# A linear-attention and Fourier kernel on one core: mirror comparisons from the fourth token tile on, weight stores in the tiles between, one transposition moved into the query product

## The chip, the core and the metric

The kernel runs on one core of a Trainium2 chip. The time is device microseconds of one execution on that core; lower is better. Engines are named as in the profile: PE is TensorE's matmul, PEld its weight load, DVE is VectorE, ACT is ScalarE, POOL is GpSimd, SP is the engine whose queue issues the DMAs. An engine works through its own instructions in order and waits, through semaphores, for those of others.

## The reference

`x` is 2048 x 640 in fp32. Four layers follow each other, each added to `x`: a Fourier layer, an attention layer, and both again with the same weights.

```python
def _A_ref(x, dft_seq_re, dft_seq_im, dft_hid_re, dft_hid_im):
    a = jnp.einsum("bsd,ed->bse", x, dft_hid_re)
    b = jnp.einsum("bsd,ed->bse", x, dft_hid_im)
    return jnp.einsum("ts,bse->bte", dft_seq_re, a) - jnp.einsum("ts,bse->bte", dft_seq_im, b)
...
def _B_ref(x, wqkv, wo):                       # 32 heads of 20
    q, k, v = ...                              # x @ wqkv
    phi = lambda t: jnp.where(t > 0, t + 1, jnp.exp(t)) + 1e-6
    pq, pk = phi(q), phi(k)
    kv = jnp.einsum("bhsd,bhse->bhde", pk, v)
    z = jnp.einsum("bhsd->bhd", pk)
    num = jnp.einsum("bhqd,bhde->bhqe", pq, kv)
    den = jnp.einsum("bhqd,bhd->bhq", pq, z)[..., None] + 1e-6
    ...                                        # (num / den) @ wo
x = x + _A_ref(_layernorm(x, axis=-1), ...)
x = x + _B_ref(_layernorm(x, axis=-1), wqkv, wo)
x = x + _A_ref(_layernorm(x, axis=-1), ...)
x = x + _B_ref(_layernorm(x, axis=-1), wqkv, wo)
```

The four DFT matrices are inputs. The kernel uses their symmetries, so it has to compare them with their own mirror images; if they don't match, it takes a general path instead, which is not run here.

## The kernel before, in words

`x` lies in SBUF as 16 token tiles of 128 rows. To keep fp32 precision, a factor is split into a high half (a cast on ACT, line 133) and a low half (a subtraction, on DVE or POOL, line 134), and a product is made of three matmuls: high by high, high by low, low by high (`product`, line 158).

A layer of attention runs in stages. `keys_values` (line 263) is the one that the change touches. Its loop over token tiles `n` does, for each tile: normalise the next tile (`normed`, line 212, with the scaling at line 127 on DVE); 30 matmuls for the keys (`proj(1, x)`, line 167); phi of the keys on ACT and DVE (lines 283 to 286) and their sum on POOL (line 298); the transposition of the next tile (`chunks`, five matmuls against the identity, line 139, then the split into halves, lines 133 and 134); 30 matmuls for the queries and phi of them. The keys of tile `n + 1` read the halves that `chunks` of tile `n` makes. The transposition stands between keys and queries, except where `got` is empty: then `query` runs it after the first two of five weight chunks, through `mid`. In the kernel before, that is so for tile 0 of layer 1 alone.

The loop runs over tiles 0 to 9, and then a gram pass over the same tiles follows: for each, 30 matmuls of normalised tokens by phi of the keys (`gram`, line 239, matmuls at line 251), whose operands `gram_ready` (line 229) makes one tile ahead: a normalisation and two splits, three DVE instructions a tile. Then the same for tiles 10 to 15. `combine` (line 368) follows, and `outputs`.

Between this work stand two side jobs.

`Check` (line 1010) makes the mirror comparisons. `fetch` loads up to four tiles of 344 or 346 KB (`ck<-in_ck`, line 1035, on SP) into the four buffers of the pool `raw`; `step` compares them on DVE (lines 1043 and 1060) and, with `more`, fetches the next. The buffers come free one by one as `step` goes on, so a fetch on SP waits for DVE. The first fetch is issued at the start of `keys_values`, when the weights of the layer, which use the same four buffers, are split. `STEPS` says in which token tiles and in which gram tiles a step stands, in both layers. The comparisons keep their program order on DVE; what else stands between them a scheduler decides, by priorities that `ahead` shifts.

`save` (line 207) writes the two halves of one weight chunk to DRAM, two stores of 320 KB on SP, so that layer 1 can load them instead of splitting again (`reload`, line 201). It is called in layer 0 alone, ten times: five chunks of the keys' weights, then five of the queries'. SP's instructions stay in program order, so a store stands behind the fetch that was issued before it.

Of the kernel before, what the change touches and what calls it, by code (L numbers as in the profile page):

```python
# [28 lines left out]
NE = 6  # L29
GA, GB = 384, 256  # L30
CUT = 10
STEPS = (0, 1, 2, 3, 4, 5, 6, 11, 12), (1, 3, 5, 7, 11)

START = 's0v s1v s2v s3v s4v r0p n2v n1v n0a n3v f0p f3p s7a k2p saa sba s9a k0v d0v s5v s6v f2v k3v d3v s8v d2v x12d d1p k1p f1v r1p n6v f6p e0v a0p b0v sda n4a n7v k7p n5v k5p k6p d5v c0v d7v k4v d4v d6v f5p r2p b1p nav kap n9v dap sfa nba dbv kbp n8a f7p f4v x03d x23d x13d x22d x02d f8v d8v a1v c1v k9p k8p f9p fap d9v b2v sca sea r3p fbv nev nfv fev a2v c2v x33a nca kcp fcv nda x32a w00a dfp dcp kfp kdp ffv fdv y32p kep dep a3v ddv v00v b3v c3v y33p t0p w12a w01a v01v v12v h3a l3v w10a v10v w02a t1p z0v v02v t3p t2p u20v u21v u22v u30v p0p w11a P0a m0v Q0v u31v u32v p1p v11p x01a y01p x11d x00a M0a N0v x10d y00v m1v'
SECOND = 'w02a sda x02d x12d x03d x13d x23a sev nea dev sfv nfa dfp nda kep kdp fdp fep x32a v02v ffv kfv y23v ddv y32v a3v x22a y22v b3p c3v h3a x33a w01a v01v y33v x10a y10v l3v t3p p1v m1p P1a w00a w10a w11a v10v u20v v11v u30v u21v u22v u31v x00d x01d M1a v00p w12a v12p x11a u32v y11p Q1p N1p'
# [114 lines left out]
def halves(pu):  # L150
    return pu.rearrange("p (a b) -> p a b", a=2)[:, :, :HD]


def h2(t):
    return t.rearrange("p (a b) -> p a b", a=2)


def product(nc, pu, sh, sl, wh, wl, hs=range(2), cs=None):
    n, m = len(sh), sh[0].shape[1]
    for c in range(n) if cs is None else cs:  # L160
        for s, w, first, last in (
            (sh[c], wh[c], c == 0, False),
            (sh[c], wl[c], False, False),
            (sl[c], wh[c], False, c == n - 1),
        ):
            for h in hs:
                nc.tensor.matmul(  # L167
                    pu[:m, 512 * h : 512 * h + HD], s, w[:, HD * h : HD * h + HD], start=first, stop=last
                )


class Attention:
# [90 lines left out]
    def keys_values(self, check=None, keep=1, saves=()):  # L263

        saves = list(saves)
        k, nc, W = self.k, self.k.nc, self.W
        pksum = k.temp()
        nc.gpsimd.memset(pksum, 0.0)
        self.PQ, late = {}, []
        if check is not None:  # L270
            check.fetch()

        def proj(part, x, mid=None):
            pu = k.psum()
            for cs in (range(ND),) if mid is None else (range(2), range(2, ND)):
                product(nc, pu, *x, [w[0] for w in W[part]], [w[1] for w in W[part]], cs=cs)
                if mid is not None and cs[0] == 0:
                    mid()
            return pu

        def phi(pu, out):
            e = k.temp()
            nc.scalar.activation(h2(e), halves(pu), AF.Relu, scale=-1.0)  # L283
            nc.scalar.activation(h2(out), halves(pu), AF.Relu)
            nc.scalar.activation(e, e, AF.Exp, scale=-1.0)  # L285
            nc.vector.scalar_tensor_tensor(out, e, 1e-6, out, op0=ALU.add, op1=ALU.add)  # L286

        x, acc, tail = self.x0, [], None
        for a, b in ((0, CUT), (CUT, NT)):
            pks = []  # L290
            for n in range(a, b):
                with k.ahead("normed", n + 1):
                    xn = self.normed(n + 1) if n + 1 < NT else None
                pk = self.slot()
                pu = proj(1, x)
                with k.ahead("key", n):
                    phi(pu, pk)
                nc.gpsimd.tensor_tensor(pksum, pksum, pk, op=ALU.add)  # L298
                pks.append(pk)
                def chunks(xn=xn, n=n):  # L300
                    tp = k.transposed(xn)
                    with k.ahead("chunks", n):
                        return k.split_chunks(tp)

                def query(i=self.order[n], x=x, mid=None):
                    pq = k.pqp.tile([128, D], F32, tag="pq", name=k.nm("pq"))
                    pu = proj(0, x, mid)
                    with k.ahead("query", i):
                        phi(pu, pq)
                    self.PQ[i] = pq  # L310

                got = []
                if xn is not None and (n or not k.layer):
                    got.append(chunks())
                if n < NT - keep:
                    query(mid=None if got or xn is None else lambda: got.append(chunks()))
                else:
                    late.append(query)
                if n > 0 and saves:
                    self.save(*saves.pop(0))  # L320
                if check is not None and n in STEPS[0]:
                    check.step(True)
                if n == b - 2:
                    with k.ahead("gram", a):
                        ready = self.gram_ready(a, pks[0])
                if xn is not None:
                    x = got[0]
            G = [k.psum() for _ in range(3)]
            tail = tail or k.psum()
            for n in range(a, b):  # L330
                with k.ahead("gram", n + 1):
                    nxt = self.gram_ready(n + 1, pks[n + 1 - a]) if n + 1 < b else None
                self.gram(G + [tail], ready, n == a, n == b - 1, a == 0)
                if n == CUT:
                    self.total(G, pksum)
                if check is not None and n in STEPS[1]:
                    check.step(n != STEPS[1][-1])
                ready = nxt
            if a == 0:
                acc = [self.slot() for _ in range(ND)]  # L340
                for c in range(ND):
                    (nc.scalar.copy if c % 2 else nc.vector.tensor_copy)(acc[c][:, :GA], self.place(G, c, 0))
                nc.scalar.copy(acc[ND - 1][:, GA:], self.place(G, ND - 1, 1))
        self.total_out(G)
        for c in range(ND):
            nc.vector.tensor_tensor(acc[c][:, :GA], acc[c][:, :GA], self.place(G, c, 0), op=ALU.add)
        c = ND - 1
        nc.vector.tensor_tensor(acc[c][:, GA:], acc[c][:, GA:], self.place(G, c, 1), op=ALU.add)
        for c in range(ND - 1):
            nc.scalar.copy(acc[c][:, GA:], self.place([None] * 3 + [tail], c, 1))  # L350
        self.combine(acc, late)
# [1002 lines left out]
```

## Time and profile before

| | us |
|---|---|
| runs of the kernel before | 807.38, 808.27, 809.39; median 808.27 |
| the profiled execution | 809.36, of which its span is 807.6 |
| layer 0, keys and queries of tiles 0 to 9 | 99.4 to 198.4 |
| layer 0, gram pass over them | 198.4 to 242.6 |
| layer 1, keys and queries of tiles 0 to 9 | 495.0 to 579.7 |
| layer 1, gram pass over them | 579.7 to 623.9 |

A row of a timeline has the start in us from the start of the span, the length, engine, line, operation, what it writes and reads, shape, count, and in brackets the idle time of the engine just before it with what ended it. A row of the chain of waits has start, length and what ran, or what was waited for. The rows themselves stand with the prediction.

### The profile page before, as it was taken

Reading aid. Unit: us, or ns where it says so; the run is one execution under the profiler, and the core shown is the slowest. Engines: PE = TensorE matmul, PEld = TensorE weight load, DVE = VectorE, ACT = ScalarE, POOL = GpSimd, SP = SyncE. Lnnn points to the kernel's source line nnn. Section 1 sums busy time; section 2 is a strip of 40 time slices with the busy share of each in tenths; the row PEclk is TensorE's granted clock in tenths of the full one; section 3 lists DMA queues with packets and bytes.
Section 4 is the critical chain, followed back from the end, with each engine's and each line's share of the span. In section 5 each row is a group of like instructions: output and inputs, shape, how many; then the busy total and the mean of one; then the engine's idle time right before and its main releaser. Section 6 shows DMA issues by size and latency. Waiting matters only on the chain.

```text
span 807.6 us, 12984 instructions
## 1 busy us (share of the span) xinstructions
PE 746.9 (92%) x4920; PEld 709.8 (88%) x4920; DVE 608.8 (75%) x1153; ACT 338.0 (42%) x592; POOL 319.1 (40%) x354
## 2 busy tenths in 40 slices
PE   0489998999999999999889999999999999999997
PEld 0138898999999999899885899999999999989997
DVE  7799887864982755999986789776597386499982
ACT  4534544355334453445563424544633445341110
POOL 4987981221021110469997656211101111134310
PEclk9989999999999999999999999999999999999999
DMA  8122416772360422000004652554044024001121
GB/s 320 64 79 73 130 57 195 248 222 105 107 204 4 141 82 80 16 8 1 1 1 134 210 174 97 176 157 141 1 140 140 1 71 143 21 12 50 66 83 70
DMA packets 36008, 81.25 MB, mean 101 GB/s; under 512 B 4142, under 2 KB 5937, under 8 KB 35936
## 3 DMA queue, kind: packets, MB, share of 16 engines
q1 hardware_dynamic: 35904, 80.27, 31.5%
q8 instruction: 41, 0.67, 0.4%
q14 instruction: 31, 0.25, 0.1%
q0 software_dynamic: 32, 0.06, 0.1%
HBM read 68.10 MB, written 11.80 MB: 99 GB/s over the span
## 4 chain that ended last, share of the span: by engine, by line
PE 64%; DVE 17%; POOL 11%; issue 3%; ACT 2%; DMA 2%; SPq 0%; DVEq 0%; POOLq 0%; ACTq 0%
PE ps L167 40%; PE ps L251 16%; PE ps L139 3%; PE ps L943 2%; PE ps L396 2%; DVE x L970 1%; DVE w L134 1%; DMA ck<-in_ck 1%; POOL ab L744 1%; POOL ab L619 1%; POOL t L440 1%; PE ps L898 1%; DVE junk L1060 1%; DVE t L134 1%; POOL ab L749 1%
## 5 line engine op out<-in xcount | busy, mean ns | idle before, releaser
L167 PE MATMUL ps<-w,t 128*128 128x320 f32 x2880 | 443.4, 312 | 8.9 <-DVE t L134 7.3
L167 PEld LDWEIGHTS ps<-w,t 128*128 128x128 f32 x2880 | 426.1, 189 | 11.8 <-DVE t L134 9.3
L298 POOL TENSOR_TENSOR t<-t,s 128x640 f32<-128x640 f32 x32 | 57.5, 1796 | 225.9 <-DVE s L286 217.9
L251 PE MATMUL ps<-t,t 128*128 128x256 f32 (+1 forms) x640 | 139.9, 309 | 0.0
L283 ACT ACTIVATE t<-ps 128x640 f32<-128x640 f32 x64 | 45.2, 706 | 162.2 <-PE ps L167 162.2
L1060 DVE CUSTOM_DVE_ANT_0 junk<-ck,ck 128x688 bf16<-128x688 f32 (+4 forms) x138 | 101.0, 732 | 10.4 <-DMA ck<-in_ck 8.6
L251 PEld LDWEIGHTS ps<-t,t 128*128 128x128 f32 x640 | 107.4, 188 | 0.0
L251 PE MATMUL ps<-w,t 128*128 128x384 f32 (+1 forms) x320 | 98.7, 310 | 0.0
L440 POOL TENSOR_TENSOR t<-pq,t 128x640 f32<-128x640 f32 x32 | 56.1, 1758 | 101.4 <-ACT t L366 48.5
L134 DVE TENSOR_TENSOR t<-ps,t 128x640 fp32r<-128x640 f32 (+1 forms) x66 | 53.9, 818 | 43.5 <-ACT t L133 43.2
L898 PE MATMUL ps<-cw,ab 128*107 128x512 f32 (+4 forms) x108 | 43.6, 544 | 33.6 <-DVE ab L639 27.0
L133 ACT CAST t<-ps 128x640 fp32r<-128x640 f32 (+1 forms) x66 | 45.6, 692 | 67.3 <-PE ps L139 58.8
L898 PEld LDWEIGHTS ps<-cw,ab 128*107 128x107 f32 (+1 forms) x108 | 19.0, 187 | 52.8 <-issue 50.3
L251 PEld LDWEIGHTS ps<-w,t 128*128 128x128 f32 x320 | 60.2, 188 | 0.2
L286 DVE SCALAR_TENSOR_TENSOR pq<-t,pq 128x640 f32<-128x640 f32 x32 | 27.2, 850 | 41.1 <-ACT t L285 41.1
L943 PE MATMUL ps<-t,u 107*128 107x322 f32 (+1 forms) x306 | 48.9, 315 | 3.2 <-DVE u L924 1.8
L943 PEld LDWEIGHTS ps<-t,u 107*128 107x128 f32 (+1 forms) x306 | 45.8, 190 | 5.6 <-DVE u L924 2.9
L139 PE MATMUL ps<-ident,t 128*128 128x128 f32 x320 | 45.6, 273 | 2.7 <-DVE t L127 1.2
L285 ACT ACTIVATE t<-t 128x640 f32<-128x640 f32 x64 | 48.0, 750 | 0.0
L127 DVE TENSOR_SCALAR t<-x,kept 128x640 f32<-128x640 f32 x58 | 44.6, 768 | 0.9 <-PE ps L251 0.9
L134 DVE TENSOR_TENSOR t<-t,t 128x640 fp32r<-128x640 f32 x32 | 26.4, 824 | 21.7 <-ACT t L133 21.3
L139 PEld LDWEIGHTS ps<-ident,t 128*128 128x128 f32 x320 | 38.2, 140 | 4.7 <-issue 1.5
(178 smaller groups left out, 992.6 us busy)
## 6 DMA issues: line engine op xcount, KB each, us to landing
ck<-in_ck SPq DMA_DIRECT2D x48, 346.0 KB
ck<-in_ck SPq DMA_DIRECT2D x48, 344.0 KB
save<-w SPq DMA_DIRECT2D x20, 320.0 KB
w<-save SPq DMA_DIRECT2D x20, 320.0 KB
x<-in_x SPq DMA_DIRECT2D x16, 320.0 KB
out<-x SPq DMA_DIRECT2D x15, 320.0 KB
raw<-in_wqkv SPq DMA_DIRECT2D x10, 320.0 KB
s<-in_wqkv SPq DMA_DIRECT2D x10, 320.0 KB
```

The costliest lines, as they stand in the source:

```text
L133: self.nc.scalar.copy(hi, src)
L134: self.engine(pool).tensor_tensor(lo, src, hi.bitcast(F32), op=ALU.subtract)
L139: self.nc.tensor.transpose(tp[:, 128 * c : 128 * c + 128], src[:, 128 * c : 128 * c + 128], self.ident)
L167: nc.tensor.matmul(pu[:m, 512 * h : 512 * h + HD], s, w[:, HD * h : HD * h + HD], start=first, stop=last)
L251: nc.tensor.matmul(self.place(G, c, part), x[:, 128 * c : 128 * c + 128], p[:, f : f + n], start=start and i == 0, stop=stop and i == 2, s ...
L283: nc.scalar.activation(h2(e), halves(pu), AF.Relu, scale=-1.0)
L285: nc.scalar.activation(e, e, AF.Exp, scale=-1.0)
L298: nc.gpsimd.tensor_tensor(pksum, pksum, pk, op=ALU.add)
L440: k.nc.gpsimd.tensor_tensor(t1, self.PQ[self.order2[n]], self.zb, op=ALU.mult)
L898: nc.tensor.matmul(pu[:m, o : o + n], e, w[:, f : f + n], start=g == 0 and i == 0, stop=g == end and not more and i == len(both) - 1,)
L943: self.k.nc.tensor.matmul(po[:, o : o + 322], s[:m, f : f + 128], w[:m, x, :], start=first, stop=last)
L1060: i = nc.vector.tensor_tensor_reduce(k.junk[:, : a.shape[1]], b, a, 1.0, 0.0, op0, op1, o)
```

## The change

The token tiles that carry a step of comparisons change from 0 to 6, 11 and 12 to 3 to 8 and 11 to 13, in both layers; the gram tiles with a step (1, 3, 5, 7 and 11) stay. The stores, until now in token tiles 1 to 10, go to token tiles 1, 2, 9, 10 and 14 and gram tiles 0, 2, 4, 6 and 8, one pair in each. In layer 0, as in layer 1 before, tile 0 no longer transposes tile 1 between its keys and its queries but inside the query product.

```diff
-STEPS = (0, 1, 2, 3, 4, 5, 6, 11, 12), (1, 3, 5, 7, 11)
+STEPS = (3, 4, 5, 6, 7, 8, 11, 12, 13), (1, 3, 5, 7, 11)
+SAVES = (1, 2, 9, 10, 14), (0, 2, 4, 6, 8)
...
                 got = []
-                if xn is not None and (n or not k.layer):
+                if xn is not None and n:
                     got.append(chunks())
                 if n < NT - keep:
                     query(mid=None if got or xn is None else lambda: got.append(chunks()))
                 else:
                     late.append(query)
-                if n > 0 and saves:
+                if n in SAVES[0] and saves:
                     self.save(*saves.pop(0))
                 if check is not None and n in STEPS[0]:
                     check.step(True)
...
                 self.gram(G + [tail], ready, n == a, n == b - 1, a == 0)
+                if n in SAVES[1] and saves:
+                    self.save(*saves.pop(0))
                 if n == CUT:
                     self.total(G, pksum)
                 if check is not None and n in STEPS[1]:
                     check.step(n != STEPS[1][-1])
...
+        assert not saves
         self.total_out(G)
```

## The prediction

> **What bounds the kernel now.** I read the page first, then busy time by stage, then TensorE's own timeline for its gaps, then what each gap waited for.
>
> ```profile
> span 807.6 us, 12984 instructions
> PE 746.9 (92%) x4920; PEld 709.8 (88%) x4920; DVE 608.8 (75%) x1153; ACT 338.0 (42%) x592; POOL 319.1 (40%) x354
> 99.39:198.40 99.01, 95.77 (x652) 94.98 (x652) 71.78 (x142) 44.28 (x70) 33.98 (x30) 0.98 0.55 172
> 198.40:242.60 44.20, 44.20 (x303) 44.10 (x302) 37.06 (x81) 17.92 (x28) 4.70 (x11) 1.00 0.49 143
> 495.00:579.70 84.70, 83.86 (x583) 83.79 (x583) 59.44 (x127) 41.22 (x65) 19.80 (x16) 1.00 0.39 118
> 579.70:623.90 44.20, 44.20 (x302) 44.13 (x302) 37.67 (x87) 17.92 (x28) 4.42 (x11) 1.00 0.43 128
> ```
>
> The stage rows give length, then busy time of PE, PEld, DVE, ACT and POOL, then the granted TensorE clock, the DMA share and GB/s. Rows one and two are layer 0's first ten token tiles and the gram pass over them, rows three and four the same of layer 1. All four are TensorE stages. Both gram passes have no gap; layer 1's token tiles have 0.84 us, at the very start, before anything the change touches. Only layer 0's token tiles lose something: 3.24 us of gaps, and a clock of 0.98. So that stage, 99 to 198 us, is where this change can win, and the other three are where it can lose.
>
> ```profile
> 99.39 4.65 PE L167 MATMUL ps<-w,t 128*128 128x320 f32 x30
> 105.27 0.74 PE L139 MATMUL ps<-ident,t 128*128 128x128 f32 x5 [1.22 <-DVE t L127]
> 105.76 9.09 PE L167 MATMUL ps<-w,t 128*128 128x320 f32 x60
> ...
> 141.28 5.62 PE L167 MATMUL ps<-w,t 128*128 128x320 f32 x26 [2.00 <-DVE t L134]
> 146.74 0.71 PE L139 MATMUL ps<-ident,t 128*128 128x128 f32 x5
> 147.20 9.01 PE L167 MATMUL ps<-w,t 128*128 128x320 f32 x60
> 156.04 0.71 PE L139 MATMUL ps<-ident,t 128*128 128x128 f32 x5
> ```
>
> Each row of five is the transposition of the next token tile; around it stand 30 key and 30 query matmuls. Between 147.20 and 156.04, 60 of them take 8.84 us, so 0.147 each, and a tile takes 9.3 us. Two gaps stand out: 1.22 us, where the second token tile isn't normalised yet, and 2.00 us, where the low half of a transposed tile isn't split yet. The 26 matmuls after the second gap take 146.74 - 141.28 = 5.46 us instead of 26 x 0.147 = 3.82: another 1.64 us. That is the clock:
>
> ```profile
> 101.61:105.02 3.41, 2.43 (x17) 2.17 (x15) 3.41 (x5) 0.89 (x2) 3.41 (x4) 1.00 0.38 106
> 139.16:142.57 3.41, 1.42 (x10) 1.29 (x10) 3.38 (x9) 1.50 (x3) 0.00 (x0) 1.00 0.82 264
> 142.57:145.99 3.42, 3.42 (x15) 3.42 (x14) 3.42 (x7) 0.00 (x0) 1.55 (x1) 0.50 0.76 190
> 391.74:395.16 3.42, 1.26 (x11) 1.00 (x9) 3.42 (x5) 1.04 (x3) 3.42 (x5) 1.00 0.00 0
> 395.16:398.57 3.41, 3.41 (x13) 3.41 (x14) 3.41 (x4) 2.23 (x5) 3.25 (x3) 0.50 0.00 0
> ```
>
> After a slice of 3.41 us with TensorE busy for only 1.42 (or 1.26) of it, the next slice is granted half the clock: 15 matmuls instead of some 23. The starts 142.57 and 395.16 lie 252.59 us apart, 74 times 3.413, so the slices seem to sit on a fixed grid. The slice with most of the 1.22 us gap was busy for 2.43 and cost no clock.
>
> Why was the split late?
>
> ```profile
> 134.75 0.70 ACT L133 CAST t<-ps 128x640 fp32r<-128x640 f32 x1
> 131.09 1.78 DVE L1060 CUSTOM_DVE_ANT_0 junk<-ck,ck 128x692 bf16<-128x692 f32 x1 [0.67 <-DMA ck<-in_ck]
> 138.68 0.88 DVE L1060 CUSTOM_DVE_ANT_0 junk<-ck,ck 128x692 bf16<-128x692 f32 x1 [1.86 <-DMA ck<-in_ck]
> 140.41 0.82 DVE L134 TENSOR_TENSOR t<-ps,t 128x640 fp32r<-128x640 f32 x1
> 149.53 0.82 DVE L134 TENSOR_TENSOR t<-ps,t 128x640 fp32r<-128x640 f32 x1
> 126.10 4.86 DMA ck<-in_ck
> 134.44 4.11 DMA ck<-in_ck
> ```
>
> The high half was cast by 135.45, but the low half began on DVE at 140.41, behind comparisons (L1060) that waited in order for their DMA. DVE had fallen behind at the start, and each late step fetched its successor late. One tile period on, at 149.53, the split is early enough for the key matmuls at 147.20 + 30 x 0.147 = 151.6, and no gap follows.
>
> **The change part by part.** *Transposition.* The order of instructions shows tile 1's five transposes after 14 query matmuls instead of before them; nothing is added.
>
> ```profile
> 103.29 1.83 DVE L127 TENSOR_SCALAR t<-x,kept 128x640 f32<-128x640 f32 x1
> 106.82 0.82 DVE L134 TENSOR_TENSOR t<-ps,t 128x640 fp32r<-128x640 f32 x1 [0.63 <-ACT t L133]
> 93.65 4.83 POOL L134 TENSOR_TENSOR w<-raw,w 128x640 fp32r<-128x640 f32 x3
> 102.97 1.79 POOL L134 TENSOR_TENSOR w<-raw,w 128x640 fp32r<-128x640 f32 x1
> ```
>
> TensorE finishes the keys at 104.04. The query weights of the first three chunks are split by 98.48 and the last at 104.76, before its turn, so it goes on at once; 14 matmuls later, at 106.1, the tile is long normalised (105.12). The 1.22 us go. Next in line is the split: transposed by 106.85, cast (0.70) and split (0.82) by 108.4. The keys of tile 1 start at 104.04 + 30 x 0.147 + 0.49 (the transposition, 105.76 - 105.27) = 108.9 and need the low half four matmuls later, at 109.5: 1.1 us of cover. If that cover were gone, up to 1.2 us return.
>
> *Comparisons.* Nine steps in layer 0's and layer 1's token tiles stay nine; they move from tiles 0 to 6, 11, 12 to tiles 3 to 8, 11, 12, 13.
>
> ```profile
> L1060 DVE CUSTOM_DVE_ANT_0 junk<-ck,ck 128x688 bf16<-128x688 f32 (+4 forms) x138 | 101.0, 732 | 10.4 <-DMA ck<-in_ck 8.6
> L1043 DVE TENSOR_REDUCE ca<-ck 128x1 f32<-128x344 f32 (+1 forms) x30 | 13.0, 433 | 0.0
> 111.70 0.49 DVE L106 BATCH_NORM_STATS2 st<-x 128x6 f32<-128x320 f32 x1 [2.18 <-POOL x L977]
> 119.21 0.80 DVE L134 TENSOR_TENSOR t<-ps,t 128x640 fp32r<-128x640 f32 x1
> ```
>
> A step is about 138/30 x 0.732 + 0.433 = 3.8 us of DVE. Without them in tiles 0 to 2, DVE is ahead from where POOL lets it go on (111.70). The tightest split there, now 119.21 to 120.01, loses two comparisons and the reduction ahead of it (1.9 us) and ends near 118.1; tile 2's keys start near 108.9 + 9.3 = 118.2 and need it 0.6 later. Thin, with some 0.7 us of cover; a miss costs up to 0.5. At tile 3 the first step's four raw tiles have been fetched since before tile 0, so the 2.00 us of waiting have no source; with them go the 1.64 us of half clock. From there each step has a whole tile period of 9.3 us, as tile 5 had when it caught up. Steps at tiles 7, 8 and 13 lie in stages with DVE idle for a quarter of the time or more (71.78 of 99.01 and 59.44 of 84.70): nothing; if a step there delayed a split, the nearest row is the gap of 2.00.
>
> *Stores.* Ten pairs of stores stay ten. On SP's queue two pairs (tiles 1 and 2) now stand right behind the first fetch, where SP waits for nothing and nothing behind them is due; two (tiles 9 and 10) stand where no fetch is near; the pair of tile 14 stands behind the fetch of tile 13's step and ahead of the loads of V's weights, which wait for TensorE anyway. Five pairs move into layer 0's gram pass, between the fetches. What they can cost is a fetch's landing in the gram pass, where DVE's queue is fuller:
>
> ```profile
> 198.47 44.06 PE ps L251 x300
> 212.74 0.33 SPq L1035 DMA_DIRECT2D ck<-in_ck  x1
> 213.36 0.50 DVE L1043 TENSOR_REDUCE ca<-ck 128x1 f32<-128x344 f32 x1
> 215.97 0.88 DVE L1060 CUSTOM_DVE_ANT_0 junk<-ck,ck 128x688 bf16<-128x688 f32 x1 [0.57 <-DMA ck<-in_ck]
> 217.29 0.82 DVE L134 TENSOR_TENSOR w<-s,t 128x640 fp32r<-128x640 f32 x1
> 221.82 0.51 DVE L1043 TENSOR_REDUCE ca<-ck 128x1 f32<-128x344 f32 x1
> ```
>
> A fetch alone lands in 215.97 - 212.74 = 3.2 us; the two in the chain above, with stores behind them, took 4.11 and 4.86. So a step may wait 0.9 to 1.6 us longer. A step's loop on DVE is 221.82 - 213.36 = 8.46 us, two gram tiles on TensorE are 8.81. With stores the loop is 9.4 to 10.1, so DVE loses 0.6 to 1.3 us in each of three loops, 1.7 to 3.8. The cover: the split at 217.29 ends at 218.11 and serves the sixth gram tile, which starts at 198.47 + 5 x 4.41 = 220.5: 2.4 us. Cost: 0 to 1.4; I take 0: of a step's four fetches only the last two have stores close behind, and the loop of 8.46 holds 0.57 of waiting already.
>
> *Sum.* 1.22 + 2.00 + 1.64 = 4.86 us. The profiled execution took 809.36 us (its span 807.6 and 1.8 around it), so it would take 804.5. The runs shown have a median of 808.27, 1.09 below, from 807.38 to 809.39, and may not all have paid the half clock: a gap of 2.00 us lies wholly inside one slice of 3.41 in (3.41 - 2.00)/3.41 = 41% of placements, and how much of it must lie inside isn't shown (between busy 1.42 and 2.43). I take half of 1.64 for the median: 808.27 - 3.22 - 0.82 = **804.2 us**. Bounds: 805.05 without the clock, 803.4 with all of it, and 802.6 if the other half-clock slice (395.16) also falls away by its place on the grid, worth about half of the 1.64 where DVE sets the pace. Upwards, 1.4 of the gram pass and part of the 0.5 of tile 2's split: 806.8. Range 802.6 to 806.8.
>
> [...]
>
> **The rivals.** *Stall moved:* the wait comes back at the new first steps, as the split at tile 3 still stands behind four wide comparisons on DVE. Then only the first gap goes: 808.27 - 1.22 = 807.05. Against it: the four raw tiles are there, and tile 5's row at 149.53. *Stores in the gram pass (slower):* if two stores behind a fetch double its landing to 6.5 us, the loop is 8.46 + 3.3 = 11.7, and three loops lose (11.7 - 8.81) x 3 - 2.4 = 6.4: 810.6 us. It decides against the change from a landing of 5.7 us (loop 10.96, loss 4.05); the rows with stores behind stop at 4.86. *Not what it says:* DVE is held at the start by POOL's residual sums (the 2.18 us before 111.70), not by comparisons, so nothing but order changes and both gaps stay in another form: 808.3. For it speaks only the thin cover at tile 2.
>
> **How the numbers follow.** Forecast 0.70, stall moved 0.13, no effect 0.09, stores 0.08. About 0.3% (2.4 us, so 805.85) is what a measurement of this kernel can tell from no change. Of the forecast's 0.70 some 0.64 lies below 805.85, and a part of the moved stall too if the clock slice goes: faster 0.68; same 0.25; slower 0.07.
>
> **What would show it.** No gap at tile 1's transposition; no gap and no half-clock slice between 130 and 150 us, so that the gram pass starts 4 to 5 us earlier, near 193.5; DVE's waits for ck gone from the token tiles. Wrong: a TensorE gap behind the splits of tiles 2 or 3, gaps in the gram pass behind the L134 splits with ck waits over 2 us, or new half-clock slices later that eat what was won.

## The result, and the profile after

The changed kernel takes 805.21 us (median of five executions, 803.95 to 805.39), the kernel before 808.27 (807.38 to 809.39). The ratio is 0.9945, with a 95% interval of 0.9929 to 0.9961: faster by about 0.5%. It is not the quotient of these two medians (0.9962); which executions it comes from isn't known here. Timed again, beside 31 executions of the kernel before with a median of 809.16 us, the changed kernel took 805.22 us, at a ratio of 0.9954 (0.9938 to 0.9971).

First the head of the page after, then busy time by stage of the profiled execution: layer 0's first ten token tiles, the gram pass over them, and the same two of layer 1. The columns are those of the prediction's stage rows.

```profile
span 803.5 us, 12981 instructions
PE 744.2 (93%) x4920; PEld 706.5 (88%) x4920; DVE 612.6 (76%) x1153; ACT 337.7 (42%) x592; POOL 317.7 (40%) x354
98.48:192.05 93.57, 93.57 (x651) 93.49 (x651) 64.42 (x127) 44.26 (x70) 33.66 (x30) 1.00 0.33 106
192.05:237.03 44.98, 44.53 (x302) 44.01 (x301) 39.05 (x86) 17.86 (x28) 5.58 (x11) 1.00 0.71 214
480.56:575.02 94.46, 93.62 (x652) 93.29 (x651) 62.79 (x137) 45.90 (x74) 27.49 (x34) 1.00 0.30 95
575.02:619.80 44.78, 44.54 (x303) 44.27 (x302) 39.82 (x89) 17.81 (x28) 5.29 (x11) 1.00 0.48 151
```

The third row begins at layer 1's first key matmul. In the kernel before, that matmul starts at 484.92 us, and not at 495.0, where the table of stages and the prediction's row for layer 1 begin; this is the kernel before from 484.92 on:

```profile
484.92:579.54 94.62, 93.78 (x653) 93.46 (x652) 69.52 (x152) 45.92 (x74) 27.99 (x34) 1.00 0.39 121
```

In the first stage TensorE is now busy for 93.57 of 93.57 us, at a clock of 1.00. From the first key matmul to the first gram matmul the kernel before took 98.92 us, so the stage is 5.35 us shorter. TensorE's own timeline shows both gaps closed:

```profile
98.48 6.76 PE L168 MATMUL ps<-w,t 128*128 128x320 f32 x44
105.08 0.71 PE L140 MATMUL ps<-ident,t 128*128 128x128 f32 x5
105.54 7.03 PE L168 MATMUL ps<-w,t 128*128 128x320 f32 x46
112.41 0.71 PE L140 MATMUL ps<-ident,t 128*128 128x128 f32 x5
...
131.12 0.71 PE L140 MATMUL ps<-ident,t 128*128 128x128 f32 x5
140.47 0.71 PE L140 MATMUL ps<-ident,t 128*128 128x128 f32 x5
```

The first transposition stands after 44 matmuls (30 keys, 14 queries), and from tile 2 on the tiles follow each other every 9.3 us with no bracket, so with no idle time. DVE's waits for ck in these tiles, 5.5 us in the kernel before, are gone.

The gram pass, without a gap before, has one now. The rows are of TensorE, of DVE, of the fetch (two issues, 214.6 and 215.0) and of the weight loads:

```profile
223.90 0.45 PE L252 MATMUL ps<-w,t 128*128 128x384 f32 x1 [0.36 <-DVE w L135]
221.69 0.88 DVE L1064 CUSTOM_DVE_ANT_0 junk<-ck,ck 128x688 bf16<-128x688 f32 x1 [3.69 <-DMA ck<-in_ck]
L1039 SPq DMA_DIRECT2D ck<-in_ck x2: 328/376/424, 214.6 to 215.0; - x2
197.32 0.19 PEld L252 LDWEIGHTS ps<-w,t 128*128 128x128 f32 x1 [0.35 <-DVE w L135]
```

DVE waited 3.69 us for a fetch that landed 221.69 - 215.0 = 6.7 us after its issue, and the split behind it came 0.36 us too late. In the second tile of the pass a weight load waited 0.35 us for a split, too. The pass grew from 44.06 to 44.98 us.

The two profiled executions differ by 807.6 - 803.5 = 4.1 us of span. By stage (before minus after): first matmul of the kernel 0.89 earlier; token tiles 5.35; gram pass -0.92; from there to layer 1's first key matmul 242.54 - 243.53 = -0.99; layer 1's token tiles 0.16; from its gram pass to the end -0.45.

### The profile page after: what moved, and what is told of

The parts are those of the page before. It is cut to its first block, busy times and chain, and to the rows that moved or that the text cites. A ratio compares the mean times of both kernels' runs of the same rounds, so it can differ in the third digit from the quotient of the medians.

```text
span 803.5 us, 12981 instructions
## 1 busy us (share of the span) xinstructions
PE 744.2 (93%) x4920; PEld 706.5 (88%) x4920; DVE 612.6 (76%) x1153; ACT 337.7 (42%) x592; POOL 317.7 (40%) x354
## 4 chain that ended last, share of the span: by engine, by line
PE 64%; DVE 21%; POOL 5%; DMA 3%; ACT 3%; issue 3%; SPq 0%; DVEq 0%; POOLq 0%; ACTq 0%
PE ps L168 44%; PE ps L252 13%; PE ps L140 3%; PE ps L947 3%; DVE w L135 2%; DVE t L135 2%; DVE junk L1064 1%; DMA ck<-in_ck 1%; DVE x L974 1%; DVE den L457 1%; POOL ab L623 1%; DVE t L461 1%; PE ps L400 1%; DMA rawc<-in_so 1%; DMA x<-in_x 1%
## 5 line engine op out<-in xcount | busy, mean ns | idle before, releaser
L1064 DVE CUSTOM_DVE_ANT_0 junk<-ck,ck 128x688 bf16<-128x688 f32 (+4 forms) x138 | 98.6, 714 | 7.3 <-DMA ck<-in_ck 5.5
L134 ACT CAST t<-t 128x640 fp32r<-128x640 f32 x32 | 23.3, 729 | 36.6 <-DVE t L128 31.8
```

What stands on the lines that cost most here:

```text
L134: self.nc.scalar.copy(hi, src)
L1064: i = nc.vector.tensor_tensor_reduce(k.junk[:, : a.shape[1]], b, a, 1.0, 0.0, op0, op1, o)
```

## The experiments

The theory was that three things add: the transposition closes the gap of 1.22 us, moving the comparisons off the first tiles closes the 2.00 us, and the half-clock slice goes with it. The rivals were that the stores behind the fetches made the split late, and that one gap was the other's echo. The table has each profiled execution's stages in us, cut at the first key matmul, the first gram matmul, the end of the gram pass and the same of layer 1; the last column is the ratio to the kernel before, timed beside it. Beside the experiments the kernel before had medians of 809.29, 809.16 and 809.90 us, so the ratios are not quotients with 808.27.

| | token tiles | gram pass | to layer 1's keys | its gram pass to the end | median | ratio (95%) |
|---|---|---|---|---|---|---|
| before | 98.92 | 44.06 | 242.54 | 228.04 | 808.27 | |
| changed | 93.57 | 44.98 | 243.53 | 228.49 | 805.21 | 0.9945 (0.9929 to 0.9961) |
| transposition alone | 96.91 | 44.16 | 243.39 | 227.87 | 808.20 | 0.9994 (0.9983 to 1.0006) |
| steps alone | 94.98 | 44.35 | 242.48 | 228.68 | 806.45 | 0.9967 (0.9954 to 0.9981) |
| stores alone | 97.18 | 44.07 | 243.38 | 228.46 | 810.13 | 1.0004 (0.9987 to 1.0021) |
| changed, stores off the gram pass | 93.58 | 44.34 | 243.06 | 228.53 | 804.39 | 0.9939 (0.9923 to 0.9955) |
| changed, again | 93.57 | 44.34 | 241.95 | 228.53 | 805.22 | 0.9954 (0.9938 to 0.9971) |
| early steps, no store near | 96.55 | 44.07 | 241.91 | 228.03 | 807.54 | 0.9978 (0.9964 to 0.9993) |
| changed, steps from tile 1 | 93.58 | 44.08 | 243.31 | 228.07 | 804.28 | 0.9940 (0.9919 to 0.9962) |
| changed, all stores in the gram pass | 93.58 | 44.60 | 242.71 | 228.62 | 805.74 | 0.9960 (0.9945 to 0.9976) |
| changed, first step in tile 0 | 94.89 | 44.05 | 242.51 | 227.97 | 805.57 | 0.9948 (0.9932 to 0.9963) |
| no step in tile 0, old transposition | 94.98 | 44.09 | 243.21 | 227.85 | 805.11 | 0.9950 (0.9936 to 0.9964) |
| two edits | 93.57 | 44.08 | 242.30 | 227.96 | 804.17 | 0.9939 (0.9923 to 0.9956) |
| steps from tile 1, stores off the gram pass | 93.57 | 44.08 | 242.97 | 227.90 | 804.48 | 0.9939 (0.9925 to 0.9954) |

### One part at a time

The transposition alone:

```diff
-                if xn is not None and (n or not k.layer):
+                if xn is not None and n:
```

> The kernel before with only the transposition of tile 1 moved into the query product. Theory (three causes add: the transposition pays for the gap of 1.22 us at 105 us, the moved comparisons for the gap of 2.00 us and the half-clock slice behind it): the gap at tile 1's transposition is gone, the gap behind the split at tile 5 and its late comparisons stay; 808.27 - 1.22 = 807.05 us, ratio 0.998 to 0.999. Rival (the start is what makes DVE late, and the gap at tile 5 is only its echo): with tile 1 transposed later, DVE is relieved, the gap of 2.00 us goes too, and the time is near that of the changed kernel, 805.2 us.

TensorE's timeline of that kernel:

```profile
105.23 0.71 PE L139 MATMUL ps<-ident,t 128*128 128x128 f32 x5
...
119.35 4.08 PE L167 MATMUL ps<-w,t 128*128 128x320 f32 x26 [1.07 <-DVE t L134]
...
140.10 4.07 PE L167 MATMUL ps<-w,t 128*128 128x320 f32 x26 [1.45 <-DVE t L134]
```

The gap at 105 us is gone, but a new one of 1.07 us stands behind the split of tile 2, and the one at tile 5 remains. Alone the edit gives nothing that can be measured (0.9994, the interval holds 1). Neither account had this: TensorE arrives earlier at a DVE that is just as late. That the gap at tile 5 remains refutes the account of it as an echo.

The steps alone:

```diff
-STEPS = (0, 1, 2, 3, 4, 5, 6, 11, 12), (1, 3, 5, 7, 11)
+STEPS = (3, 4, 5, 6, 7, 8, 11, 12, 13), (1, 3, 5, 7, 11)
```

> The kernel before with only the steps of the comparisons moved to tiles 3 to 8 and 11 to 13; stores in tiles 1 to 10 as before, the transposition as before. Theory (DVE's queue behind the early comparisons makes the split of tile 5 late): the gap of 2.00 us and its half-clock slice are gone, the gap of 1.22 us stays, and the gram pass has no gap, since no store stands in it; 808.27 - 2.00 - 0.82 = 805.45 us, ratio 0.9965. Rival (stores behind the fetches make the fetches land late, and that makes the split late): a gap of 1 to 2 us comes back at one of tiles 3 to 8, where fetches and stores still share the queue; 807 to 808.3 us.

The gap at tile 5 is gone with the stores of tiles 3 to 8 still behind the fetches; the gap at tile 1 (1.20 us here) is the only one between 100 and 190 us. The ratio of 0.9967 is what the theory gave (0.9965).

The stores alone (`SAVES` as in the changed kernel, the rest as before):

> The kernel before with only the stores moved (tiles 1, 2, 9, 10, 14 and gram tiles 0, 2, 4, 6, 8); steps in tiles 0 to 6, 11, 12 and the transposition as before. Theory (the early steps are the cause, the stores only add to the landing of a fetch): the fetches of tiles 3 to 6 land in about 3.2 us instead of 4.1 to 4.9, but the splits still wait behind comparisons; a gap of 0.5 to 2.0 us stays behind tile 4 or 5, the gap of 1.22 us stays too; 807 to 808.5 us, and a gap of up to 0.7 us in the gram pass. Rival (stores are the cause): no gap between 110 and 198 us but the 1.22, no half-clock slice there; 805.5 us.

```profile
140.32 4.08 PE L168 MATMUL ps<-w,t 128*128 128x320 f32 x26 [2.00 <-DVE t L135]
135.59:139.00 3.41, 2.73 (x19) 2.47 (x17) 1.40 (x5) 1.22 (x3) 0.00 (x0) 1.00 0.97 335
139.00:142.42 3.42, 2.10 (x14) 2.10 (x15) 3.42 (x9) 0.70 (x2) 0.65 (x1) 1.00 0.82 228
142.42:145.83 3.41, 3.41 (x27) 3.40 (x26) 3.38 (x6) 1.39 (x3) 0.91 (x1) 1.00 0.68 211
```

The first row is TensorE's, the others its clock slices. The same gap of 2.00 us stands in the same place, so moving the stores does nothing by itself. But the stores of tiles 1 and 2 still lie beside the early fetches here, so the run is no clean test of the rival. It prices the half clock instead: the gap falls on two of the slices of 3.41 us, busy for 2.73 and 2.10 us, neither costs any clock (1.00 in each and behind them), and the 26 matmuls behind it take 4.08 us where the kernel before took 5.62. The median of 810.13 us (807.39 to 812.48) lies above the 807 to 808.5 of the theory, but the kernel before took 809.29 (806.77 to 812.63) beside it, and the interval of the ratio holds 1; the profiled execution took 808.22.

The clean test: early steps and the old transposition, but no store before tile 7.

```diff
+SAVES = (7, 8, 9, 9, 10, 10, 13, 13, 14, 14), ()
...
-                if n > 0 and saves:
+                for _ in range(SAVES[0].count(n) if saves else 0):
                     self.save(*saves.pop(0))
...
```

> Comparisons in tiles 0 to 6, 11, 12 and the transposition of tile 1 as in the kernel before, but no store before tile 7 (one pair each in tiles 7 and 8, two each in 9, 10, 13, 14, none in the gram pass). Theory (the early steps keep DVE behind, whatever lies on the queue): the waits for ck among the comparisons of tiles 3 and 4 get shorter, by 1 to 2 us in sum, but a gap of 0.3 to 2.0 us stays at tile 4, 5 or 6, and the 1.22 us stay; 806.5 to 808.3 us. Rival (the stores near the fetches make the splits late): no gap behind a split between 110 and 198 us; 805.5 to 806.3 us.

```profile
105.46 0.74 PE L140 MATMUL ps<-ident,t 128*128 128x128 f32 x5 [1.19 <-DVE t L128]
...
140.63 4.09 PE L168 MATMUL ps<-w,t 128*128 128x320 f32 x26 [1.29 <-DVE t L135]
```

DVE's waits for ck in these tiles add up to 3.9 us, against 5.5 in the kernel before, as forecast. The gap is 1.29 instead of 2.00 us. So the early steps make a gap with no store near. Whether the other 0.71 us belong to the stores isn't shown by one execution each: the run of the stores alone had 2.00 us, the transposition alone 1.45.

### Which of the early steps

The changed kernel with its steps in tiles 1 to 6 and 11 to 13:

> The changed kernel with the steps in tiles 1 to 6 and 11 to 13 instead of 3 to 8 and 11 to 13; stores and transposition as in the changed kernel. Theory (what makes the split late is what DVE has to do while it catches up after the residual sums, so a step in tiles 1 and 2 is already too early): a gap of 0.5 to 2 us behind the split of one of tiles 2 to 5 comes back; 806 to 807.5 us. Rival (it is tile 0's step alone, or the number of steps, that matters): no gap, 805.2 us.

The theory falls: no gap, 93.58 us, as with steps from tile 3. Steps in tiles 1 and 2 were not too early. Then tile 0's step is left. Two runs look at it from both sides: tile 0's step put back, with the others late,

```diff
-STEPS = (3, 4, 5, 6, 7, 8, 11, 12, 13), (1, 3, 5, 7, 11)
+STEPS = (0, 3, 4, 5, 6, 7, 11, 12, 13), (1, 3, 5, 7, 11)
```

> The changed kernel with its first step back in tile 0 and the others in tiles 3 to 7 and 11 to 13. It parts what tile 0's step does by its own work on DVE from what it does through the fetches behind it. Theory (its comparisons fall into the time in which DVE and GpSimd still finish the residual sums, and push the split of tile 2; the gap at tile 5 is a second thing, made by late fetches of the steps that follow at once): a gap of about 1.0 us behind the split near 118 us, as with the transposition moved alone (1.07), and none at tiles 4 to 6; 805.2 + 1.0 = 806.2 us. Rival (only the run of steps from tile 0 on is too much, one step there is harmless): no gap between 100 and 198 us; 804.3 to 805.2 us.

and tile 0's step alone taken away, with the stores and the transposition as in the run of the stores alone (steps in tiles 1 to 6 and 11 to 13):

> The kernel with steps in tiles 1 to 6 and 11 to 13 and the stores of the changed kernel, but with tile 1 transposed between keys and queries as before. Beside the run with the stores moved alone it differs only in tile 0's step; beside the run with steps from tile 1 only in the transposition. Theory (two separate gains, one in front of the other): the gap of 1.2 us at 105 us stays and is the only one up to 198 us; 804.3 + 1.2 = 805.5 us. Rival (the transposition's 1.2 us only shift TensorE against DVE and are absorbed later): the gap is there, but the gram pass starts no later after the first key matmul than with the transposition moved; 804.3 us.

With tile 0's step put back, TensorE's gap and DVE's queue ahead of it are these:

```profile
119.45 4.08 PE L168 MATMUL ps<-w,t 128*128 128x320 f32 x26 [1.09 <-DVE t L135]
113.44 1.66 DVE L287 SCALAR_TENSOR_TENSOR pq<-t,pq 128x640 f32<-128x640 f32 x1
115.03 0.32 DVE L1047 TENSOR_REDUCE ca<-ck 128x1 f32<-128x173 f32 x1
115.27 0.86 DVE L1064 CUSTOM_DVE_ANT_0 junk<-ck,ck 128x692 bf16<-128x692 f32 x1
...
116.26 0.82 DVE L1064 CUSTOM_DVE_ANT_0 junk<-ck,ck 128x692 bf16<-128x692 f32 x1
...
118.59 0.80 DVE L135 TENSOR_TENSOR t<-ps,t 128x640 fp32r<-128x640 f32 x1
```

The same stretch of DVE in the changed kernel, whose first key matmul is 0.23 us earlier:

```profile
113.19 1.66 DVE L287 SCALAR_TENSOR_TENSOR pq<-t,pq 128x640 f32<-128x640 f32 x1
...
116.59 0.81 DVE L135 TENSOR_TENSOR t<-ps,t 128x640 fp32r<-128x640 f32 x1
117.32 0.82 DVE L287 SCALAR_TENSOR_TENSOR s<-t,s 128x640 f32<-128x640 f32 x1
```

One reduction and two comparisons stand ahead of the split: 118.59 - 116.59 - 0.23 = 1.77 us, enough for a gap of 1.09 at tile 2, and no gap follows at tile 5. Taking tile 0's step away brings 97.18 - 94.98 = 2.20 us, all of the gap at tile 5, while the 1.20 at tile 1 stay. With it go all of DVE's waits for ck in the token tiles. The first row is from the run of the stores alone (total, number, longest wait); the run without tile 0's step has no such row. The second is TensorE's only gap in that run between 100 and 190 us:

```profile
DVE junk L1064 <- DMA ck<-in_ck: 5.1, 6, 1.5
104.50 0.74 PE L140 MATMUL ps<-ident,t 128*128 128x128 f32 x5 [1.20 <-DVE t L128]
```

So tile 0's step does two things: by its own work it pushes the split of tile 2, and at the head of an unbroken run of steps it makes the later fetches late enough for a gap at tile 5. Whether taking out another step of that run would close the gap at tile 5 as well, no run shows. The transposition's price, with nothing late behind it, is 94.98 - 93.58 = 1.40 us. These prices rest on the stages of single traces. The ratios of whole executions can't tell these kernels apart: 0.9948 and 0.9950 for the two runs above, whose stage is 1.3 and 1.4 us longer than that of the changed kernel, 0.9945 and 0.9954 for the changed one.

### The stores in the gram pass

Two pairs in each of tiles 1, 2, 9, 10 and 14, none in the gram pass, the rest as in the changed kernel (`SAVES = (1, 1, 2, 2, 9, 9, 10, 10, 14, 14), ()`):

> The changed kernel with two pairs of stores in each of tiles 1, 2, 9, 10 and 14 and none in the gram pass. Theory (stores behind the fetches make the gap of 0.36 us at 224 us in the gram pass): that gap is gone and a fetch there lands in about 3.2 us again; 805.21 - 0.4 to 0.7 = 804.5 to 804.8 us. Rival (that gap comes from where the steps stand, since the first gram step now follows steps at tiles 7 and 8): it stays, 805.2 us. Against both: four stores in a row at tile 1 or 2 hold the first fetch or a load of weights back, and a new gap appears there; over 805.5 us.

The changed kernel once more:

> The changed kernel once more, for a second profile and for times on the same chip as the next three. Theory (the gap of 0.36 us at 224 us in the gram pass comes from the two stores behind a fetch, and so belongs to the kernel, not to one execution): a wait for ck of 2 us or more and a gap of 0.2 to 0.8 us near 224 us again; 805.2 us. Rival (an accident of one execution): no gap there. The two gaps of 0.75 and 0.80 us between 427 and 443 us, where a part of the gain was lost, come back if they belong to the kernel and not to the execution.

All ten pairs in the gram pass, two behind each fetch (`SAVES = (), (0, 0, 2, 2, 4, 4, 6, 6, 8, 8)`):

> The changed kernel with all ten pairs of stores in the gram pass, two pairs behind each fetch in gram tiles 0, 2, 4, 6 and 8, none in the token tiles. It prices the rival of the prediction (stores in the gram pass lengthen the fetches). Theory (only the fetch that is issued just ahead of the stores, one of the four of a step, lands late, and DVE's queue gives back part of it): the longest wait for ck grows from 3.7 to 6 to 7.5 us and the gaps in the gram pass from 0.36 to 3 to 5 us; 807.5 to 810 us. Rival of that (the stores take bandwidth from every fetch, as the prediction's rival had it: each of three loops loses): waits for ck of over 5 us in three steps, gaps of 10 us or more; over 814 us. Third (the gap does not come from the stores): no change, 805.2 us.

Without stores the gap is gone, the waits for ck add up to 0.8 us, and 804.39 us is close to what the theory gave. But it is gone from the second execution of the changed kernel as well; there the same fetch kept DVE waiting 1.30 us. And with twice the stores TensorE has no gap either, and the time is 805.74 us, not 807.5 or more. The waits of these two kernels on DVE, the changed one again and the one with all stores in the pass:

```profile
220.26 0.88 DVE L1064 CUSTOM_DVE_ANT_0 junk<-ck,ck 128x688 bf16<-128x688 f32 x1 [1.30 <-DMA ck<-in_ck]
```
```profile
210.71 0.88 DVE L1064 CUSTOM_DVE_ANT_0 junk<-ck,ck 128x688 bf16<-128x688 f32 x1 [0.55 <-DMA ck<-in_ck]
221.02 0.88 DVE L1064 CUSTOM_DVE_ANT_0 junk<-ck,ck 128x688 bf16<-128x688 f32 x1 [1.60 <-DMA ck<-in_ck]
230.45 0.87 DVE L1064 CUSTOM_DVE_ANT_0 junk<-ck,ck 128x688 bf16<-128x688 f32 x1 [2.00 <-DMA ck<-in_ck]
```

So the 0.36 us were a chance of one execution. Stores made fetches late: in the seven traces with stores in the pass DVE's waits for ck from 193 to 245 us add up to 2.2 to 4.7 us, in the seven without to 0.6 to 1.1. How late differs from one execution to the next: 4.7 and 2.7 us in the two of the changed kernel. The pass covered single waits of up to 2.37 us (the run without tile 0's step) with no gap of TensorE, and all but 0.36 of the 3.69. What does belong to the kernel is smaller. The five runs whose last early step stands in tile 8 have 44.34 us or more, the others 44.05 to 44.16 with or without stores: some 0.27 us, for the weight load that waits in the pass's second tile. The kernel with its first step in tile 0, which differs from the changed one only in that tile 8's step stands in tile 0, is among the others (44.05). From layer 1's gram pass on, the same five take 228.49 to 228.68, the others 227.85 to 228.07, except the stores alone (228.46).

### Joined variants

Two edits on the kernel before, the stores untouched:

```diff
-STEPS = (0, 1, 2, 3, 4, 5, 6, 11, 12), (1, 3, 5, 7, 11)
+STEPS = (1, 2, 3, 4, 5, 6, 11, 12, 13), (1, 3, 5, 7, 11)
...
-                if xn is not None and (n or not k.layer):
+                if xn is not None and n:
```

> The kernel before with two edits only: tile 0's step moved to tile 13 and the transposition of tile 1 moved into the query product; stores in tiles 1 to 10 as before, and so behind the fetches. Theory (tile 0's step and the transposition are all that the change needed): no gap between 100 and 198 us but at the very start, none in the gram pass; 804.3 to 805.2 us, ratio 0.994 to 0.9955. Rival (the stores had to move too, since they lengthen the fetches: without a store near, the gap at tile 5 was 1.29 instead of 2.00 us): a gap of 0.3 to 1.0 us behind the split of tile 3, 4 or 5; 805.5 to 806.2 us.

Steps from tile 1 joined with the stores off the gram pass:

> Steps in tiles 1 to 6 and 11 to 13, the transposition moved, and two pairs of stores in each of tiles 1, 2, 9, 10 and 14, none in the gram pass: the two variants that came out lowest, joined. Theory (nothing is left to win in these stages, as both already ran without a gap between 100 and 242 us): 804.3 us, no faster than either. Rival (the stores cost something still in the gram pass, and the later steps in the token tiles): 803.5 us or less. Against both: four stores behind the fetch of tile 1's step make the comparisons of tile 2 late, and a gap comes back at tile 3 or 4; over 805 us.

Both have 93.57 and 44.08 us, TensorE has no gap in either stage once the keys have begun, and both times lie within 0.2 us of the theory's. The two edits alone take 804.17 us, the lowest median of all: the stores did not have to move. By its interval (0.9923 to 0.9956) it can't be told from the changed kernel; by the stages of the traces it is 0.3 to 0.9 us shorter in layer 0's gram pass and 0.5 us shorter from layer 1's gram pass on.

## Why the prediction was right, and where it was not

*Direction and place* were right: the stage of layer 0's token tiles carries the gain, both named gaps are closed, and so is the half-clock slice. The stage gained 5.35 us where the sum had 4.86. Its terms, as the runs part them in the order stores, tile 0's step, transposition (they add up to the whole by construction): 1.40 for the transposition (1.22 forecast), 2.20 for the split at tile 5 (2.00), and, for the half clock (1.64), 98.92 - 97.18 = 1.74 between the kernel before and the one with the stores alone, which has the same gap at full clock; 5.62 - 4.08 = 1.54 of it stand in the 26 matmuls behind the gap. The first two are each 0.2 us more than the gap that they close. The clock term was paid in the trace of the kernel before, where the gap left a slice with 1.42 us of matmuls, and not in that of the stores alone, where it left slices of 2.73 and 2.10; so half of it was a guess about chance, and no run counts how often an execution pays it.

*That each term can be had by itself*, as the experiments' theory read the sum, was wrong; the sum holds because the change makes all its edits at once. The 1.22 us of the transposition can only be had once tile 0's step has moved; alone, the gap comes back as 1.07 us at tile 2. This is the prediction's rival of the moved stall, in another tile and for one half of the change. The cover that the prediction called thin there, 0.7 us, is the reason, and it was sized well: with tile 0's step back TensorE was ready at 119.45 - 1.09 = 118.36 us, which is 118.13 on the changed kernel's time, and there the split ended at 117.40. Two comparisons and a reduction ahead of the split (1.9 us by the prediction, 1.77 measured) use these 0.73 us up.

*"Each late step fetched its successor late"* was right as a chain: the waits for ck of 5.1 us go with tile 0's step alone. The prediction reasoned as if tiles 0 to 2 all had to be free; freeing tile 0 was enough.

*The stores.* The prediction moved them at no cost in the token tiles and took 0 of 0 to 1.4 in the gram pass. Without stores in it the pass took 44.34 us; with them one execution of the changed kernel took 44.34, the other 44.98, and the one with twice as many 44.60: 0 to 0.64, within the bounds. The rival's 6.4 us failed at its factor: a landing of over 5.7 us, from which it was to decide, did occur (6.7), but in one of three loops, and not in every execution. With it one of the prediction's own signs of being wrong appeared, a gap in the gram pass behind a wait for ck of over 2 us, and it cost 0.36 us.

*"Steps at tiles 7, 8 and 13: nothing"* failed. The idle quarter of DVE that it leaned on is an average over the stage and says nothing of its border (and tile 13 lies in neither of the two stages that it quotes). A step in tile 8 delays operands of the gram pass, 0.27 us in layer 0. In layer 1 the five traces with such a step, and no others, show TensorE waiting 0.24 to 0.26 us for a split there, and about 0.5 us more from there on. The row of the changed kernel:

```profile
580.49 0.44 PE L252 MATMUL ps<-w,t 128*128 128x384 f32 x1 [0.24 <-DVE w L135]
```

*What was given back.* Between the gram pass and layer 1 the profiled execution was 0.99 us slower than before. TensorE's timeline there, of the changed kernel and then of its second execution:

```profile
424.14 2.80 PE L902 MATMUL ps<-cw,ab 128*107 128x512 f32 x6 [1.53 <-DMA cw<-in_co]
427.74 7.97 PE L902 MATMUL ps<-cw,ab 128*107 128x512 f32 x18 [0.80 <-DMA cw<-in_so]
...
442.03 0.95 PE L902 MATMUL ps<-ch,tl 128*107 128x512 f32 x3 [0.75 <-DVE tl L800]
```
```profile
424.67 10.52 PE L902 MATMUL ps<-cw,ab 128*107 128x512 f32 x24 [1.80 <-DMA cw<-in_co]
...
440.65 0.95 PE L902 MATMUL ps<-ch,tl 128*107 128x512 f32 x3
```

The same kernel took 243.53 and 241.95 us for this part, and the other kernels lie between 241.91 and 243.39, in no order with their edits. So the part varies by 1.6 us from execution to execution, and the change has no share in it that these runs could show. What decides a landing or a late DVE there stays open.

*The level.* 804.2 us were forecast and 805.21 measured. The sum for the median left out the tile-8 steps (0.27 and about 0.5) and took half of the clock slice, of which the trace of the kernel before shows the whole (5.62 us for 26 matmuls) and that of the stores alone nothing (4.08); the rest lies within the spread of the executions. As a ratio the forecast is 804.2 / 808.27 = 0.9950, between the two that were measured. A match this close is in part luck: the two profiled executions differ by 4.1 us, where the sum for them was 4.86, and 0.89 us gained before the stage and 0.49 more in it than the sum partly cancel the 0.92 and 0.99 lost behind it.

## What to carry to other kernels

A gap's width is what its removal brings only if the next engine in the chain is not late as well: look at when the late engine would deliver for a consumer that arrives earlier. When several pieces of side work sit in a busy start, move the first one before moving all; here one step and one transposition held the whole gain, and the pieces that went further than needed took a little of it back at the next stage's border. Before explaining a gap below 1 us, take a second trace of the same kernel.

## What the runs showed of the hardware

*The half clock went with the gap's place in its slice, and its price with the stage.* In the trace of the kernel before, the granted clock falls to 0.50 twice between 100 and 800 us, at 142.57 and at 395.16, 252.59 us or 74 times 3.413 apart; in that of the first step in tile 0, at 391.49 and at 415.38, 23.89 us or 7 times 3.413 apart. A gap of 2.11 to 2.18 us stands in layer 0's outputs in nine traces, ahead of a group of 26 matmuls that begins between 389.50 and 395.10 us. In four of them the 26 take 5.60 to 5.63 us (before, steps alone, early steps with no store near, steps from tile 1), in five 4.08 or 4.09 (changed, changed again, transposition alone, stores off the gram pass, all stores in it). These are slices of 3.41 us, each with the slice behind it, from four kernels: changed, steps from tile 1, first step in tile 0, and stores off the gram pass.

```profile
388.00:391.41 3.41, 1.91 (x13) 1.91 (x14) 3.41 (x4) 1.20 (x3) 3.33 (x4) 1.00 0.00 0
391.41:394.82 3.41, 3.30 (x25) 3.04 (x23) 3.41 (x5) 1.95 (x5) 3.33 (x4) 1.00 0.00 0
```
```profile
387.03:390.45 3.42, 1.30 (x9) 1.04 (x8) 3.42 (x5) 0.60 (x2) 3.42 (x4) 1.00 0.00 0
390.45:393.87 3.42, 3.42 (x15) 3.42 (x14) 3.42 (x4) 2.31 (x6) 3.25 (x4) 0.50 0.00 0
```
```profile
411.97:415.38 3.41, 1.85 (x12) 1.34 (x11) 2.55 (x3) 2.53 (x6) 3.33 (x5) 1.00 0.00 0
415.38:418.80 3.42, 3.42 (x15) 3.42 (x14) 2.70 (x4) 1.37 (x3) 3.26 (x4) 0.50 0.00 0
```
```profile
422.76:426.17 3.41, 1.57 (x5) 0.69 (x5) 2.69 (x7) 0.00 (x0) 0.80 (x2) 1.00 0.81 252
426.17:429.59 3.42, 3.26 (x9) 1.13 (x8) 2.39 (x6) 0.57 (x2) 2.20 (x4) 1.00 0.79 283
```

Neither column draws the border. With 1.85 us of matmul time the clock fell, with 1.57 it stayed; with 1.34 us of weight loads it fell, with 0.69 it stayed (there the Fourier layer's 128x512 matmuls begin). Among slices of attention work alone the weight-load column still parts those shown: behind 1.34 us and less the clock fell, behind 1.52 and more it stayed. The slice with 1.52 us is the changed kernel's:

```profile
398.24:401.65 3.41, 2.16 (x14) 1.52 (x12) 3.41 (x7) 3.24 (x7) 2.31 (x3) 1.00 0.00 0
401.65:405.07 3.42, 3.38 (x23) 3.38 (x24) 3.42 (x5) 2.13 (x5) 3.42 (x2) 1.00 0.01 2
```

What of a slice is counted stays open. The same gap of 2.00 us cost 1.54 us in the trace of the kernel before (5.62 against 4.08 for the 26 matmuls behind it) and nothing in that of the stores alone.

The fall at 390 us cost nothing in the end, where the prediction's range gave it half of 1.64. TensorE's rows of the kernel with steps from tile 1, then of the changed one:

```profile
389.94 5.60 PE L168 MATMUL ps<-w,t 128*128 128x320 f32 x26 [2.12 <-DVE t L135]
...
402.09 2.18 PE L168 MATMUL ps<-w,t 128*128 128x320 f32 x13 [0.46 <-DVE t L135]
```
```profile
389.50 4.08 PE L168 MATMUL ps<-w,t 128*128 128x320 f32 x26 [2.11 <-DVE t L135]
...
399.89 0.85 PE L168 MATMUL ps<-w,t 128*128 128x320 f32 x4 [0.35 <-ACT t L134]
401.69 2.48 PE L168 MATMUL ps<-w,t 128*128 128x320 f32 x15 [0.94 <-DVE t L135]
```

At half clock 402.09 - 389.94 = 12.15 us pass, at full clock 401.69 - 389.50 = 12.19: DVE, busy for 12.12 of these 12.19 us, sets the pace, and TensorE only waits less behind (0.46 us, against 0.35 and 0.94). The part from the gram pass to layer 1's keys takes 241.91 to 243.31 us in the four traces with 5.60 us or more and 241.95 to 243.53 in the five with 4.09 or less.

*The same fetch landed after 6.7 and after 4.2 us.* The fetch of 344 KB with two stores behind it had landed, as DVE's next comparison shows, after 6.7 us in one execution of the changed kernel. In the second its two issues were at 215.7 and 216.1, and DVE went on at 220.26, 4.2 us after the later one.
